# Identity on chip, k and two blocks' normalised rows turned by transfers, some sums as adding transfers: a long-convolution and FFN kernel in one planned order

## The chip, the cores and the metric

The program runs on one core of one Trainium2 chip. The core has five engines that run their own lists of instructions in order: TensorE (PE, matrix products), VectorE (DVE), ScalarE (ACT), GpSimd (POOL) and SyncE (SP, which here only issues transfers). Sixteen DMA engines move data. Time is device time in microseconds (us) of one execution. The kernel before took 301.45 us as the median of three runs (300.62 to 301.98). The profiled execution is one further run of 300.51 us, of which 298.7 us lie between its first and its last instruction (the span).

## The reference

S = 2048 positions, D = 640 channels, F = 1728, bfloat16 inputs.

```python
def _A_ref(q, k, v, shift_k, ssm_k, ssm_D):        # q is layernorm(A_q)
    k_shift = sum of 4 shifted copies of k, each times its tap shift_k[:, t]
    kv = k_shift * v
    y = causal convolution of kv with ssm_k along S (rfft, product, irfft of length 2S)
    return q * (y + kv * ssm_D)

def _B_ref(x, w_gate, w_up, w_down):
    return (silu(x @ w_gate) * (x @ w_up)) @ w_down

h   = A_q + _A_ref(layernorm(A_q), A_k, A_v, A_shift_k, A_ssm_k, A_ssm_D)
out = h + _B_ref(layernorm(h), B_w_gate, B_w_up, B_w_down)
```

## The kernel before

**Tiling.** The 2048 positions are four blocks of 512 (`NB`, `BLK`); a block's rows lie on 128 partitions, four to a partition (`R`). For block j the kernel computes kv_j (`kv_of`): k is turned on PE by products with an identity (L436), copied from PSUM to SBUF (L438), and the four taps are 20 products per row group with diagonal matrices `diag` (L450), multiplied by v on DVE (L455) or after a copy on ACT (L457, L458). The first column of the turned k is the last one of the block before; it is kept in `halo`.

**Convolution.** It is done in blocks with a transform of length 1024, written as products with a fixed basis `WF` of cosines and sines. `transform` makes the spectrum X_j of kv_j and G_j of the filter block (turned by `g_turned`). It forms two sums over even and odd rows on PE (L301), copies them out (L306), and then adds and subtracts them on DVE (L342 "lo", L339 "hi"). With `minus` (a basis with signs changed, `DIRECT`) PE makes both results itself with twice the products (L325) and DVE has no sums to do; G0 is done so. `window` joins G_j and G_{j-1} to H_j; `mac` adds up the complex products X_i H_{j-i} on DVE (L470, L492, L493). `inverse` forms the difference and the sum of the two halves on DVE (L567, L570), goes back with `WI` on PE (L582), multiplies by the normalised row (L592, with the row's sum as a by-product), adds it to x (L595), and makes the second layer norm's statistics: squares on ACT (L503), and the chain of small operations in `norm` (L510 to L532). `turn_h` normalises the rows (L547), turns them on PE with the identity (L609) and copies them to `hT` (L611).

**FFN.** `ffn(j)` runs seven groups of gate and up columns: per group two weight loads on SP (L626), products of 128x512 (L639), silu on ACT (L645), product with up (L654, L656), and then the products with `wd` (L686). For blocks 0 to 2 the block's h is first stored to the output, and the FFN's result is added to it in DRAM by a transfer with accumulation on POOL's queue (L698). The last block adds on DVE (L692) and stores from SP (L696).

**Order.** Nothing is issued when its line is reached. Every line records an operation in a `Plan`, with an engine, an assumed duration, what it reads and writes, and a priority set by `plan.line`. `Plan.schedule` then takes, again and again, the operation that can start first by its own assumed times (ties by priority), gives it a buffer of its tag (`slots`), and so writes the order of each engine's list. Buffers, and so the waits on them, follow from that order. For block j the priority is 10 j, and the FFN of block j-1 has its PE part at 10 j + 15, so it fills PE beside the convolution of block j. The identity is a constant in DRAM that is loaded on ACT's queue behind the taps (L702, L703).

Of the kernel before, what the change touches and what calls it, by code (L numbers as in the profile page):

```python
# [31 lines left out]
FLEX, DIRECT, ACTLN, ACTKV, ENDDVE = 100, ('G0',), 12, 12, True  # L32
SPLIT = ((0,), (1,))

# [34 lines left out]
class Plan:  # L69
    ISSUE = {"sp": 450, "add": 1300}  # L70
    QUEUE = {"add": "pool"}
# [8 lines left out]
    def line(self, at, **own):  # L80

        self.all, self.at = at, own
# [23 lines left out]
    def schedule(self):  # L106
        free = {"sp": 700.0, "aq": 700.0}
        idle = {t: [(0.0, i) for i in range(n)] for t, n in self.slots.items()}
        dma_free = 0.0
        todo = list(self.ops)  # L110
        order = []
        while todo:
            best = None
            for op in todo:
                if any(d.end is None for d in op.deps):
                    continue
# [3 lines left out]
                for b in op.bufs:  # L120
                    if b.tag is not None and b.at is None:
# [7 lines left out]
                        ready = max(ready, sorted(idle[b.tag])[n - 1][0])  # L129
                if not ok:  # L130
                    continue
                for way, late in [((op.eng, op.ns, op.fn), 0.0)] + ([(op.other, 1e3)] if op.other else []):
# [4 lines left out]
                    key = (at, op.prio + late, op.n)  # L137
                    if best is None or key < best[0]:
                        best = (key, op, way)
            if best is None:  # L140
                for op in todo[:60]:
                    print(op.n, op.eng, [(b.tag, b.at) for b in op.bufs], [d.n for d in op.deps if d.end is None])
                print({t: len(idle[t]) for t in idle})
# [6 lines left out]
            for b in op.bufs:  # L150
                if b.tag is not None and b.at is None:
                    idle[b.tag].sort()
                    b.at = idle[b.tag].pop(0)[1]
                    if b.tag in self.turn:
                        self.turn[b.tag].pop(0)
            op.start = start
            if op.eng in self.ISSUE:
                free[self.QUEUE.get(op.eng, op.eng)] = start + self.ISSUE[op.eng]
                dma_free = max(dma_free, start + self.ISSUE[op.eng]) + op.ns
                op.end = dma_free + 1600  # L160
# [8 lines left out]
            order.append(op)  # L169
        order.sort(key=lambda o: (o.start, o.n))  # L170
# [5 lines left out]
def kernel(ctx: ExitStack, tc: tile.TileContext, A_q, A_k, A_v, A_shift_k, A_ssm_k, A_ssm_D, B_x,  # L176
# [7 lines left out]
    slots = {"S": 8, "scr": 3, "x": 2, "ld": 3, "kT": 1, "t4": 2, "hT": 1, "tT": 1, "wgu": 2, "row": 4, "o": 1, "sg": 3,  # L184
             "ps_c": 2, "ps_f": 2, "sm": 4}
    shape = {"S": ([P, 2, 4, D], BF16), "scr": ([P, 4, D], BF16), "x": ([P, R, D], BF16), "ld": ([P, R * D], BF16),
             "kT": ([P, KT, R, P + 2], BF16), "t4": ([P, R, D], BF16), "hT": ([P, KT, BLK], BF16),
# [19 lines left out]
    def conv_ps():  # L207

        turns[0] ^= 1
        return new("ps_f" if plan.all < 2 and turns[0] else "ps_c")  # L210
# [13 lines left out]
    def evict(fn, r, w, ns=700, other=820):  # L224

        return plan.add("act", ns, lambda: fn(nc.scalar.copy), r, w, (),
                        ("dve", other, lambda: fn(nc.vector.tensor_copy)) if plan.all < FLEX else None)
# [4 lines left out]
    def load(nbytes, fn, w, r=()):  # L232
        return plan.add("sp", nbytes / 300.0, fn, r, w)

# [17 lines left out]
    id_h = nc.inline_tensor(np.eye(P, dtype=np.float32).astype(ml_dtypes.bfloat16), name="const_ident")  # L252
# [6 lines left out]
    halo = fixed([P, KT, R, 1], BF16, "halo")  # L259
# [53 lines left out]
    def transform(src, dst, pieces, minus=None):  # L313
# [19 lines left out]
        for ws in () if minus else pieces:  # L333
# [10 lines left out]
            dve(wide(1490, ws), lo, [odd], [(dst, bits((0,), ws=ws))])  # L344
# [42 lines left out]
    def spectrum(src, pieces=((0, 1),), minus=None):  # L387
        b = new("S")
        transform(src, b, pieces, minus)
        return Spec(b)  # L390

    def window(G, prev, to):

        H = Spec(new("S")) if to is None else Spec(to.b, True)
        dve(1490, lambda: nc.vector.tensor_add(H.part(0), G.part(0), prev.part(1)), [G.at(0), prev.at(1)], [H.at(0)])
# [28 lines left out]
    def kv_of(j, k, v):  # L424

        kT = new("kT")
        if j == 0:
            dve(60, lambda: nc.vector.memset(ap(kT)[:, :, :, 0:1], 0.0), [], [(kT, "halo")])
        else:
            dve(100, lambda: nc.vector.tensor_copy(ap(kT)[:, :, :, 0:1], ap(halo)), [halo], [(kT, "halo")])  # L430
        for r in range(R):
            pt = conv_ps()

            def tr(r=r, pt=pt):
                for c in range(KT):
                    nc.tensor.transpose(turned(pt)[:, c * P:(c + 1) * P], rd(k)[:, r, c * P:(c + 1) * P], ap(ident))  # L436
            pe(290, tr, [k, ident], [pt], [kT])
            evict(lambda copy, r=r, pt=pt: copy(  # L438
                ap(kT)[:, :, r, 1:P + 1], turned(pt)[:, 0:D].rearrange("p (c t) -> p c t", c=KT)), [pt], [(kT, r)], other=490)
# [361 lines left out]
```

## Time and profile before

| what | us |
|---|---|
| median of three runs | 301.45 (300.62 to 301.98) |
| the profiled execution | 300.51 |
| its span, first to last instruction | 298.7 |
| PE busy in it | 276.9 (93%) |
| DVE busy | 227.2 (76%) |
| ACT busy | 176.8 (59%) |
| POOL busy | 27.2 (9%) |
| first product on PE starts | 7.79 |
| first FFN product on PE starts | 57.45 |
| FFN of the last block starts on PE | 249.60 |
| last product's result is read by DVE | 295.13 |

Busy time counts stretches in which an engine executes; a group's mean is the length of one instruction, and neighbouring ones overlap on PE, so that 540 products of 379 ns make 122.9 us and not 204.7. The granted TensorE clock was 1.000 throughout. Idle time of an engine matters only where another one, or the end, waits for it.

### The profile page before, as it was taken

The numbers are of one execution on the slowest core, as the hardware profiler recorded it, in microseconds if no ns is written. First come the engines' busy times: TensorE is split into PE (matmuls) and PEld (weight loads), VectorE is DVE, ScalarE is ACT, GpSimd is POOL, SyncE is SP. The second block draws the span as 40 slices with busy tenths as digits, with TensorE's granted clock in tenths as the row PEclk, the third lists the DMA queues.
The fourth block names the chain that finished last, engine by engine and source line by source line (L and its number), as shares of the span: only waits on it lengthen the run. The fifth ranks groups of instructions, "written<-read, shape, count | busy, mean of one in ns | idle before, by whom it ended". The sixth has DMA issues, their size and how long they took to land.

```text
span 298.7 us, 4920 instructions
## 1 busy us (share of the span) xinstructions
PE 276.9 (93%) x1964; PEld 170.0 (57%) x1964; DVE 227.2 (76%) x315; ACT 176.8 (59%) x299; POOL 27.2 (9%) x58
## 2 busy tenths in 40 slices
PE   0899866799999999999999999999999998999995
PEld 0786644665555676665576456654446664444563
DVE  0579998998899989999698999997999871110212
ACT  1848869797775757878768644455453534544300
POOL 0000000362100001126200002110000121000000
PEclk9999999999999999999999999999999999999999
DMA  7999122517536357226242561335555232654011
GB/s 266 373 333 383 49 81 88 178 14 243 170 101 156 102 162 192 34 22 138 81 115 54 150 171 22 37 55 151 150 137 133 25 36 39 170 145 96 2 44 44
DMA packets 52089, 36.91 MB, mean 124 GB/s; under 512 B 12705, under 2 KB 49762, under 8 KB 52066
## 3 DMA queue, kind: packets, MB, share of 16 engines
q1 hardware_dynamic: 49538, 34.59, 39.5%
q0 software_dynamic: 1728, 1.97, 5.7%
q8 instruction: 15, 0.25, 0.4%
q10 hardware_dynamic: 800, 0.04, 0.2%
q14 instruction: 8, 0.07, 0.1%
HBM read 32.00 MB, written 4.59 MB: 122 GB/s over the span
## 4 chain that ended last, share of the span: by engine, by line
PE 85%; DVE 8%; ACT 3%; DMA 2%; issue 1%; ACTq 0%; DVEq 0%
PE ps_f L639 38%; PE ps_f L686 21%; PE ps_c L301 8%; PE ps_c L450 6%; PE ps_c L582 4%; DMA ident<-const_ident 2%; PE ps_f L325 1%; PE ps_c L325 1%; PE ps_f L450 1%; PE ps_c L609 1%; ACT hT L611 1%; DVE row L592 1%; DVE S L470 1%; DVE diag L715 1%; PE ps_c L354 1%; PE ps_c L436 1%
## 5 line engine op out<-in xcount | busy, mean ns | idle before, releaser
L639 PE MATMUL ps_f<-hT,wgu 128*128 128x512 bf16 x540 | 122.9, 379 | 0.7 <-DVE hT L611 0.7
L639 PEld LDWEIGHTS <-wgu 128*128 128x128 bf16 x540 | 52.0, 98 | 57.0 <-issue 0.8
L686 PE MATMUL ps_f<-wd,tT 128*128 128x320 bf16 x448 | 66.3, 300 | 0.2
L686 PEld LDWEIGHTS <-tT 128*128 128x128 bf16 x448 | 41.6, 97 | 22.4 <-issue 7.2
L645 ACT ACTIVATE sg<-ps_f 128x1024 bf16<-128x1024 f32 (+1 forms) x28 | 26.9, 962 | 26.8 <-PE ps_f L639 26.7
L656 DVE TENSOR_TENSOR tT<-sg,sg 128x1024 bf16<-128x1024 bf16 (+1 forms) x27 | 17.5, 649 | 30.7 <-ACT sg L654 30.4
L493 DVE TENSOR_TENSOR S<-S,scr 128x2560 bf16<-128x2560 bf16 x24 | 35.8, 1492 | 0.8
L654 ACT CAST sg<-ps_f 128x1024 bf16<-128x1024 f32 (+1 forms) x27 | 25.5, 946 | 17.5 <-PE ps_f L639 17.4
L301 PE MATMUL ps_c<-t,WF 128*128 128x320 bf16 x208 | 33.9, 299 | 2.0 <-DVE row L592 1.3
L492 DVE TENSOR_TENSOR scr<-S,S 128x2560 bf16<-128x2560 bf16 x24 | 35.6, 1484 | 0.0
L301 PEld LDWEIGHTS <-WF 128*128 128x128 bf16 x224 | 21.5, 98 | 14.1 <-issue 3.7
L503 ACT ACTIVATE row<-x 128x640 bf16<-128x640 bf16 x32 | 23.5, 740 | 8.0 <-DVE x L595 7.4
L698 POOL DMA_DIRECT2D out_dram<-o x12 | 10.6, 883 | 154.5 <-ACT o L694 154.5
L450 PEld LDWEIGHTS <-kT 128*128 128x128 bf16 x320 | 21.4, 107 | 3.1 <-DVE kT L438 1.2
L306 ACT CAST scr<-ps_c 128x640 bf16<-128x640 f32 (+1 forms) x28 | 17.9, 672 | 5.0 <-PE ps_c L301 5.0
L306 ACT CAST S<-ps_c 128x640 bf16<-128x640 f32 (+1 forms) x22 | 13.7, 660 | 10.2 <-PE ps_c L301 10.2
L450 PE MATMUL ps_c<-diag,kT 128*128 128x128 bf16 x280 | 18.3, 226 | 0.2 <-ACT hT L611 0.2
L582 PEld LDWEIGHTS <-WI 128*128 128x128 bf16 x128 | 12.4, 98 | 9.3 <-issue 3.6
L592 DVE SCALAR_TENSOR_TENSOR row<-row,ps_c 128x640 bf16<-128x640 bf16 x14 | 11.5, 819 | 3.2 <-PE ps_c L582 2.6
L611 ACT COPY hT<-ps_c 128x640 bf16<-128x640 bf16 x12 | 8.1, 695 | 9.5 <-PE ps_c L609 9.5
L694 ACT CAST o<-ps_f 128x640 bf16<-128x640 f32 x12 | 8.3, 693 | 8.9 <-PE ps_f L686 7.2
L539 ACT ACTIVATE row<-x 128x640 bf16<-128x640 bf16 x16 | 11.8, 740 | 1.2 <-DMA x<-in_A_q_dram 1.2
(93 smaller groups left out, 293.5 us busy)
## 6 DMA issues: line engine op xcount, KB each, us to landing
wgu<-in_B_w_gate_dram SPq DMA_DIRECT2D x24, 320.0 KB, 3.4
wgu<-in_B_w_up_dram SPq DMA_DIRECT2D x24, 320.0 KB, 3.2
ld<-in_A_k_dram SPq DMA_DIRECT2D x4, 640.0 KB, 4.1
x<-in_A_q_dram SPq DMA_DIRECT2D x4, 640.0 KB, 5.2
ld<-in_A_v_dram SPq DMA_DIRECT2D x4, 640.0 KB, 6.8
ld<-in_A_ssm_k_dram SPq DMA_DIRECT2D x4, 640.0 KB, 6.7
wd<-in_B_w_down_dram SPq DMA_DIRECT2D x1, 2080.0 KB, 11.1
out_dram<-x SPq DMA_DIRECT2D x3, 640.0 KB, 3.8
```

The costliest lines, as they stand in the source:

```text
L301: nc.tensor.matmul(ap(ps)[:, w, 0:NH], ap(WF)[:, r, c, :], ap(src)[:, r, w * NH:(w + 1) * NH], start=(i == 0), stop=(i == 1))
L306: copy(two(cut(to(c)[2](), ws)) if len(ws) == 2 else cut(to(c)[2](), ws), half(ap(ps)) if len(ws) == 2 else ap(ps)[:, ws[0], 0:NH])
L450: nc.tensor.matmul(line(ap(ps))[:, c * P:(c + 1) * P], ap(kT)[:, c, q, off:off + P], ap(diag)[:, 4 * c + t, :], start=(t == 0), stop=(t == 3))
L492: nc.vector.tensor_mul(flat2(b), X.part(xs), H.part(hs))
L493: f(A.part(dst), A.part(dst), flat2(b))
L503: act(930, lambda r=r, junk=junk: nc.scalar.activation(ap(junk), ap(x)[:, r, :], ACT.Square, scale=D ** -0.5, accum_out=sm(s, 1)[:, r:r + ...
L582: nc.tensor.matmul(ap(ps)[:, w, 0:NH], m, src[:, w * NH:(w + 1) * NH], start=(i == 0), stop=(i == len(terms) - 1))
L639: nc.tensor.matmul(ap(ps)[:, i, :], ap(w)[:, k, off:off + P], ap(hT)[:, k, :], start=(k == 0), stop=(k == KT - 1))
L645: act(580 * n + 20 if n == 1 else 1010, lambda: nc.scalar.activation(ap(sg)[:, 0:n, :], ap(gate[0])[:, gate[1]:gate[1] + n, :], ACT.Silu), ...
L654: nc.scalar.copy(ap(co)[:, 0:n, :], ap(up[0])[:, up[1]:up[1] + n, :])
L656: op.rest = dve(420 if n == 1 else 690, lambda: nc.vector.tensor_mul(ap(tT)[:, c:c + n, :], ap(sg)[:, 0:n, :], ap(co)[:, 0:n, :]), [sg, co ...
L686: nc.tensor.matmul(ap(ps)[:, hf, 0:NH], ap(tT)[:n, c, r * P:(r + 1) * P], ap(wd)[:n, c, hf * NH:(hf + 1) * NH], start=(c == 0), stop=(c == ...
```

## The change

It has these parts.

- **Identity.** No longer loaded: DVE sets a tile to one, POOL keeps its diagonal (L806, L807). The taps move to the head of SP's queue (L805), ahead of k.
- **k by transfers.** For blocks 1 to 3, four transfers per block that transpose on the way write k turned into `kT` (L465); block 0 is still turned on PE (L476). `kT` has two buffers; the column from the block before is copied by POOL (L487), and `halo` and its copies on DVE are gone.
- **Rows of blocks 2 and 3 by transfers.** `turn_h` issues a transposing transfer per row (L664) in place of L609 and L611.
- **Sums by adding transfers** on POOL's queue (`add_into`, L260): the "lo" sum for G1, X1, G2 and X2, the sum of the window for H2, and x + row for block 2's four rows.
- **Norms on GpSimd**: the second layer norm of blocks 1 and 2.
- **More by PE alone**: block 0's inverse is in `DIRECT` (64 products in place of 32, no sums on DVE).
- **ACT as first choice** for normalising the rows of block 1 in the convolution, for block 1's copy before the product with v, and for the rows of the second norm of blocks 2 and 3.
- **The last block's last row** of the output is finished in two halves of 320 columns.
- **Order.** Each stage of each block gets its own offset to its priority (`PLACE`); the planner's assumed times for transfers change, a buffer that was taken counts from when it came free, and, of several operations that could start first on an engine, one with a priority lower by 5 or more is taken. `SLOTS`: x from 2 to 1, ld 3 to 2, kT 1 to 2, row 4 to 5, o 1 to 3, sm 4 to 6. `ROWS` are worked off as 1, 3, 0, 2.
- `LEAD`, `ADDMAC` and `WAIT` are empty or zero, so the paths they switch on are not taken.

```diff
-FLEX, DIRECT, ACTLN, ACTKV, ENDDVE = 100, ('G0',), 12, 12, True
+ADDLO, ADDMAC, ADDWIN, ADDH, LEAD = ('G1', 'X1', 'G2', 'X2'), (), (1,), (2,), {}
+PAD = 16
+DIRECT, ACTLN, ACTKV, ACTLN2 = ('G0', 'inv0'), 1, 1, (2, 3)
+LN1DVE, LN2POOL, HTURN = (0,), (2, 1), (2, 3)
+WAIT = {'dve': 0, 'act': 0, 'pe': 0}
+PLACE = {"G0": 14.5, "G1": 2.5, "G2": -71.0, "G3": -15.5, "X0": -14.5, "X1": -10.5, "X2": -13.5, "X3": 15.0,
...
+SLOTS = {"S": 8, "scr": 3, "x": 1, "ld": 2, "kT": 2, "t4": 2, "hT": 1, "tT": 1, "wgu": 2, "row": 5, "o": 3,
+         "sg": 3, "ps_c": 2, "ps_f": 2, "sm": 6}
+ROWS = (1, 3, 0, 2)
...
-    ISSUE = {"sp": 450, "add": 1300}
-    QUEUE = {"add": "pool"}
+    ISSUE = {"sp": 450, "turn": 1260, "add": 870}
+    QUEUE = {"turn": "sp", "add": "pool"}
...
+            best = min(found, key=lambda f: f[0]) if found else None
+            if best:
+                until = best[0][0] + WAIT.get(best[2][0], 0)
+                best = min((f for f in found if f[2][0] == best[2][0] and f[0][0] <= until and (f[0][1] <= best[0][1] - 5 or f is best)),
+                           key=lambda f: (f[0][1] // 5, f[0][0], f[0]))
...
+    def add_into(to, what, r, w, n=R * D):
+
+        plan.add("add", 2 * P * n * 2 / 375.0, lambda: nc.gpsimd.dma_start(
+            out=to(), in_=what(), accum_op=ALU.add, max_dma_last_dim=2 * D * 2), r, w)
...
             dve(wide(1490, ws), hi, [odd, (dst, bits((0,), ws=ws))], [(dst, bits((1,), ws=ws))])
-            dve(wide(1490, ws), lo, [odd], [(dst, bits((0,), ws=ws))])
+            if name in ADDLO:
+                add_into(lambda: ap(dst)[:, 0], lambda odd=odd: ap(odd), [odd], [(dst, bits((0,)))])
+            else:
+                dve(wide(1490, ws), lo, [odd], [(dst, bits((0,), ws=ws))])
...
+        if to and ADDWIN:
+            add_into(lambda: prev.part(1), lambda: G.part(0), [G.at(0), prev.at(1)], [H.at(0)])
+        else:
+            dve(1490, lambda: nc.vector.tensor_add(H.part(0), G.part(0), prev.part(1)), [G.at(0), prev.at(1)], [H.at(0)])
...
+    def load_k(j):
+
+        kT = new("kT")
+        if j == 0:
+            load(MB, lambda: nc.sync.dma_start(out=plain(kT), in_=block(kk, j)), [kT])
+        for r in range(R) if j else ():
+            plan.add("turn", MB / 4 / 300.0, lambda r=r: nc.sync.dma_start(
+                out=ap(kT)[:, :, r, PAD:], in_=block(kk, j)[:, r, :], transpose=True), [], [(kT, r)])
+        return kT
...
-            dve(100, lambda: nc.vector.tensor_copy(ap(kT)[:, :, :, 0:1], ap(halo)), [halo], [(kT, "halo")])
+            plan.add("pool", 900, lambda: nc.gpsimd.tensor_copy(ap(kT)[:, :, :, PAD - 1:PAD], ap(before)[:, :, :, PAD + P - 1:]),
+                     [(before, r) for r in range(R)], [(kT, "halo")])
...
+                if plan.block in ADDH:
+                    add_into(lambda r=r: ap(x)[:, r, :], lambda t=t: ap(t), [t], [(x, r)], D)
+                else:
+                    dve(490, lambda r=r, t=t: nc.vector.tensor_add(ap(x)[:, r, :], ap(x)[:, r, :], ap(t)), [t], [(x, r)])
...
-        norm(s, nc.vector, n1)
+            norm(s, nc.gpsimd if plan.block in LN2POOL else nc.vector, n1, bias=True, rs=sorted(rs))
...
+            if plan.block in HTURN:
+                plan.add("turn", MB / 4 / 300.0, lambda hn=hn, at=at: nc.sync.dma_start(
+                    out=ap(hT)[:, :, at * P:(at + 1) * P], in_=ap(hn), transpose=True), [hn], [(hT, r)])
+                continue
...
+            last = end and r == ROWS[-1]
+            for lo, hi in zip(cuts, cuts[1:]):
+                for hs in ((0,), (1,)) if last else ((0, 1),):
...
-    plan.add("aq", 1900, lambda: nc.scalar.dma_start(out=ap(tapw), in_=A_shift_k.rearrange("(c p) t -> p c t", p=P)), [], [tapw])
-    plan.add("aq", 1900, lambda: nc.scalar.dma_start(out=ap(ident), in_=id_h.ap()), [], [ident])
-    k = load_t(kk, 0)
+    load(1e3, lambda: nc.sync.dma_start(out=ap(tapw), in_=A_shift_k.rearrange("(c p) t -> p c t", p=P)), [tapw])
+    dve(100, lambda: nc.vector.memset(ap(ident), 1.0), [], [ident])
+    plan.add("pool", 1500, lambda: nc.gpsimd.affine_select(ap(ident), ap(ident), [[-1, P]], ALU.is_equal, 0.0, base=0, channel_multiplier=1), [], [ident])
+    k = load_k(0)
```

## The prediction

> **What bounds the kernel now.** I read the page's busy times and slices first, then the busy time of four stretches, the start's timeline, the end of block 0's convolution, and the groups that the change touches.
>
> ```profile
> PE 276.9 (93%) x1964; PEld 170.0 (57%) x1964; DVE 227.2 (76%) x315; ACT 176.8 (59%) x299; POOL 27.2 (9%) x58
> ...
> PE   0899866799999999999999999999999998999995
> ```
>
> ```profile
> core 0: us, PE busy (x) PEld busy (x) DVE busy (x) ACT busy (x) POOL busy (x), PEclk, DMA share, GB/s
> ...
> 7.80:57.40 49.60, 40.64 (x365) 31.10 (x365) 43.01 (x83) 39.06 (x89) 0.49 (x2) 1.00 0.63 215
> 57.40:226.00 168.60, 168.52 (x1191) 100.70 (x1189) 157.58 (x183) 111.51 (x176) 23.07 (x49) 1.00 0.46 113
> 226.00:295.20 69.20, 67.75 (x414) 38.12 (x412) 25.79 (x50) 24.96 (x36) 3.48 (x4) 1.00 0.32 72
> ```
>
> There are two regimes. To 57.4 us the kernel waits for loads and then walks block 0's chain through DVE, ACT and PE. From there PE is the bound: 0.08 us idle in the third stretch, 1.4 us up to its last product. DVE is nearly full beside it to 226 us (93%) and almost free after.
>
> ```profile
> 4.50 0.10 PEld L436 LDWEIGHTS <-ld 128*128 128x128 bf16 x1 [4.50 <-DMA ld<-in_A_k_dram]
> 7.79 0.69 PE L436 MATMUL ps_f<-ident,ld 128*128 128x128 bf16 x5 [7.79 <-DMA ident<-const_ident]
> 7.84 2.82 DVE L715 TENSOR_TENSOR diag<-ident,tapw 128x2560 bf16<-128x2560 bf16 x1 [6.90 <-DMA ident<-const_ident]
> ...
> 38.55 0.81 DVE L567 TENSOR_TENSOR scr<-S 128x1280 bf16<-128x1280 bf16 x1
> ...
> 47.81 0.49 DVE L595 TENSOR_TENSOR x<-x,row 128x640 bf16<-128x640 bf16 x1
> ...
> 52.07 1.51 DVE L547 TENSOR_SCALAR row<-x,sm 128x640 bf16<-128x640 bf16 x4
> ...
> 57.45 0.81 PE L639 MATMUL ps_f<-hT,wgu 128*128 128x512 bf16 x3
> ```
>
> k is there at 4.50 but the identity only at 7.79; the inverse's sums start on DVE at 38.55, its last row is done at 48.30, the norm at 52.03, the first FFN product starts at 57.45.
>
> ```profile
> L436 PE MATMUL ps_c<-ident,ld 128*128 128x128 bf16 x70 | 6.3, 232 | 0.5 <-ACT scr L306 0.3 <-ACT kT L438 0.2
> L609 PE MATMUL ps_c<-ident,row 128*128 128x128 bf16 x70 | 5.6, 220 | 1.6 <-ACT hT L611 1.6
> L342 DVE TENSOR_TENSOR S<-S,scr 128x2560 bf16<-128x2560 bf16 x5 | 7.5, 1491 | 0.1
> L698 POOL DMA_DIRECT2D out_dram<-o x12 | 10.6, 883 | 154.5 <-ACT o L694 154.5
> q0 software_dynamic: 1728, 1.97, 5.7%
> ```
>
> PE's turning costs 0.08 to 0.09 us a product, a "lo" sum 1.49 us of DVE, an adding transfer 0.88 us of POOL.
>
> **The change, part by part**, against the profiled span of 298.7 us.
>
> *Start.* k is turned when both k and the identity are there. Both are uncertain. k is now queued behind the taps: the identity, 32 KB, queued behind the same taps, landed 6.5 us after its issue, k, 640 KB at the head, 3.8 us after its own; so k lands between 5.0 (0.45 us for one issue more) and about 8.5. The identity needs a memset and one POOL operation. POOL's rows of 128x4 run from 0.19 to 1.5 us, POOL is idle from 0.43 us, and nothing in the trace bounds a first operation there from above, so I put it between 1.5 and 8.5. Turning starts between 5.0 and 8.5 in place of 7.79: a gain of 2.8 to a loss of 0.7. I take 6.8, the middle: **-1.0**. `diag` (2.82 us) goes along, since it too waits for taps and identity.
>
> [...]
>
> *Block 0's inverse on PE alone.* DVE's four sums go (38.55 to 41.82). After the last product sum in `mac`, PE does the second half's first row (8 products of 0.136, 1.1 us), then DVE takes four rows at 1.27 us (43.86, 45.13 in the old spacing): 6.8 us from the end of `mac` to the last row, against 48.30 - 38.55 = 9.75. **-2.9**. The 32 extra products (4.3 us) run while DVE makes the second half's products, where PE idles now (5.54 of 8.0 us busy from 35 to 43); without that cover they would cost up to 2.2 us for one half.
>
> *From the last row to the first FFN product.* The norm began 1.74 us after the last row, behind two copies of 0.82; in the new order two copies of 0.49 stand there: -0.3 after one more small operation of 0.17. From the norm's end to the first product it took 5.4 us, with k's four turnings, their copies and one tap group (1.28) in the way. In the new order four normalisings (1.5), three row copies on ACT (0.70 each) and two basis sums (0.55 each) end last: 4.5. **-1.2** in all. So the first FFN product moves from 57.45 to 52.4.
>
> *PE's work after it.* 1599 products before, 1544 after: 80 turnings less (40 for k, 40 for rows), 25 more that used to lie ahead (20 of the taps, 1.12 us, and 5 turnings of a filter). In full flow a pair of groups of 10 takes 0.73 us, so a turning is worth about 0.056 to 0.09: 80 of them 4.5 to 7.2, less 1.4. I take the low price, since they were interleaved: **-3.2** (to -5.8). All FFN and inverse products are the same ones.
>
> *The end.* The last row's final addition covers 320 columns in place of 640, 0.47 in place of 0.82 (L306's copy of 320 against L692): **-0.35**.
>
> *What waits instead.* PE had 1.4 us idle after the first FFN product. From DVE 14.6 us go there (four "lo" sums and a window sum of 1.49, four additions of 0.49, two norms of 2.0, the halo copies), from PE 3.2, so DVE's work has more room. But five sums of 640 KB are now transfers, and DVE waits for their end. An adding transfer of 160 KB landed 3.4 us after its issue; the queue's share (5.7% of 16 engines over the span, 272 engine-us for 1.97 MB) makes 1.4 us of data for 160 KB and 5.6 for 640, so 7.6 us; the lower end is the plain 640 KB store, 3.8 us. In the new order the places are: G1's sum has some 7 us (four products with v, paced by PE) before DVE needs it; X1's has 6.1 (0.69, two of 1.49, five of 0.49), and POOL does block 1's first norm ahead of it (3.5 and 7.8 us in the two runs before); H2's sum is issued only when G2's has landed, and DVE has 3.7 us of other work (two of 1.49, one of 0.69) before it needs H2. So 0 to 1.5 us of waiting at X1 and 0 to 4 at H2, and 0 to 3 more from POOL's order. Part is absorbed in DVE's room. I put PE's idle time at 3.2, between 0.3 and 9: **+1.8**.
>
> *Covered at nothing.* Block 2's rows: the chain is four adding transfers, squares, a POOL norm (up to 8 us), four ACT rows of 0.92, four turning transfers; PE has about 30 us of FFN work of block 1 left when the inverse ends, and the chain adds to 22 or so. The new order's POOL queue has no DRAM additions between these. Block 3's rows are the tight place: after the inverse PE has three groups of 1.08 and 112 products of 0.144 (16.12 us), some 17.2 us from the last inverse product. The chain: row and addition 1.4, square 0.93, two more small FFN products on ACT and DVE (about 2), norm 2.2, row 0.44, four transfers issued one after another, the landing. Up to the first issue that is 7.0. A turning transfer is not in the trace. Nearest below is a plain load of 160 KB, 0.37 us to issue and 3.6 to land; above, the filter load in 640 pieces, 6.7 us to land. At 1 us apiece and 4 to land it is 15.0, so 2.2 us are left. Block 1's k has over 30 us.
>
> [...]
>
> **Sum:** -1.0 - 2.9 - 1.2 - 3.2 - 0.35 + 1.8 = -6.85, span 291.9, the profiled execution 293.7. The median of the runs shown is 0.94 above the profiled one; I take half of that: 294.1.
>
> **Rivals.** *A: DVE waits for its sums.* If adding transfers take 7.6 us and more beside the weight loads, DVE falls behind by some 2 to 4 us at each of X1, G2 and H2, and PE waits for block 1's and block 2's inverse; idle 7 to 10 in place of 3.2: 298 to 301. For it: DVE at 93% before. Against: 14.6 us less to do.
>
> *B: everything is covered and the start is early.* Turning starts at 5.0 (-1.8 more) and PE idles 0.5 (-2.7 more): 289.6. For it: 0.08 us idle over 168.6 us in the old plan with a fuller DVE.
>
> *C: slower, by turning transfers.* In block 3's hand-over each microsecond per row beyond 1 costs four; 2.2 us are free and 6.85 gained, so from about 3.3 us a row the gain is gone. At the filter load's 6.7 us one after another, the four take 26.8, the FFN of block 3 starts 20.6 us late, and the kernel takes 314 or more. For it: no such row in the trace. Against: a plain load of this size lands in 3.6 with several in flight.
>
> *D: the identity is not earlier* (POOL late, or k behind the taps): the start gives nothing or loses 0.7, 295.1 to 295.8.
>
> **How the numbers follow.** Forecast with D 0.60 (about 292 to 297), B 0.14 (289 to 292), A 0.18 (297 to 301), C 0.08 (from 301). The range 289.2 to 299.6 leaves out about half of A's upper part, C, and a bit of B. Under 0.5% is about what a measurement can't tell from no change (299.9 to 303.0 is "same"): faster 0.87, same 0.05, slower 0.08.
>
> **What would show it.** Start: first product on PE near 6.8, and what it waits for. Inverse: L631 with `minus`, first FFN product near 52.4. PE: 1896 products, busy near 273. Sums: waits of DVE for a transfer into S, and PE idle between 57 and 200. Hand-over: PE waiting for hT from L664 before block 3's first FFN product would be C. The prediction is wrong if transfers into hT or S appear on the chain of work that ended last with more than 5 us.

## The result and the profile after

The changed kernel takes 303.35 us (median of eight, 302.71 to 304.97); the kernel before took 301.65 beside it (300.58 to 302.50). The ratio is 1.0073, with a 95% interval of 1.0044 to 1.0101. It is slower by 0.7%, a little more than the half per cent that the prediction called hardly measurable. 294.1 was forecast, and the measurement lies outside the range.

The profiled execution took 303.14 us, its span is 301.1. From the page of the changed kernel, the busy line, then slices:

```profile
PE 276.1 (92%) x1896; PEld 166.5 (55%) x1896; DVE 206.7 (69%) x269; ACT 174.2 (58%) x291; POOL 98.0 (33%) x103
...
PE   2999989999994999989899996699999999999995
...
POOL 0000101297001499115993798220891022000000
PEclk9999999999998999999999999599999999999999
```

PE has 68 products less, DVE 20 us less to do, and POOL 98.0 us in place of 27.2. PE now has two holes, in slice 13 (about 90 to 98 us) and around slices 25 and 26 (180 to 196), and in both the granted clock drops. POOL is full for some stretch ahead of each. Busy time by stretch of the changed kernel, from the first FFN product on:

```profile
core 0: us, PE busy (x) PEld busy (x) DVE busy (x) ACT busy (x) POOL busy (x), PEclk, DMA share, GB/s
48.30:85.00 36.70, 36.70 (x330) 24.51 (x328) 26.99 (x27) 29.43 (x49) 15.59 (x17) 1.00 0.78 171
85.00:100.00 15.00, 11.15 (x57) 6.06 (x56) 14.06 (x15) 9.20 (x14) 1.20 (x1) 0.89 0.54 108
100.00:180.00 80.00, 77.37 (x535) 46.52 (x533) 72.24 (x79) 52.06 (x87) 50.86 (x51) 1.00 0.59 130
180.00:215.00 35.00, 29.11 (x163) 15.70 (x162) 25.46 (x19) 19.87 (x34) 13.67 (x14) 0.90 0.49 96
215.00:297.58 82.58, 82.50 (x469) 44.32 (x466) 30.54 (x52) 33.58 (x44) 15.06 (x15) 1.00 0.45 97
```

Set against the prediction's terms, by the two profiled executions:

| stretch | before | after | change | forecast |
|---|---|---|---|---|
| to the end of block 0's products on DVE | 38.55 | 34.12 | -4.4 | -1.0 |
| from there to block 0's last row | 9.75 | 6.22 | -3.5 | -2.9 |
| from there to the first FFN product | 9.15 | 7.96 | -1.2 | -1.2 |
| PE busy from the first FFN product to the last product | 236.2 | 236.8 | +0.6 | -3.2 |
| PE idle in that stretch | 1.5 | 12.45 | +11.0 | +1.8 |
| from the last product to the end of the span | 3.57 | 3.52 | -0.05 | -0.35 |

The first FFN product starts at 48.30 where 52.4 was forecast, so the first half went better than foretold. All of it and more went after that. The waits of the changed kernel say at what:

```profile
ACT row L600 <- POOL sm L560: 11.3, 2, 9.4
DVE scr L539 <- DMA S<-scr: 10.5, 2, 5.3
...
PE ps_f L781 <- ACT o L786: 5.9, 1, 5.9
...
PE ps_c L631 <- DVE scr L616: 3.9, 1, 3.9
```

and POOL has come onto the chain that ended last, where it had no share before (first line before, second line changed):

```profile
PE 85%; DVE 8%; ACT 3%; DMA 2%; issue 1%; ACTq 0%; DVEq 0%
PE 52%; DVE 20%; POOL 14%; DMA 6%; ACT 3%; issue 3%; DVEq 0%; SPq 0%; ACTq 0%; POOLq 0%
```

There are two causes of waiting. ACT stands 9.4 us before block 2's rows (L600) because POOL's norm isn't done; the copy of an output of block 1's FFN (L786) is queued behind it on ACT, and PE waits 5.9 us for that copy's PSUM buffer. And DVE stands twice, for 5.3 and 5.2 us, before L539 because X1's and X2's sums, adding transfers, land late; behind the first of these PE waits 3.9 us for block 1's inverse, and the second delays block 2's inverse and so the norm that ACT waits for. Those sums were ready early. X1's was ready to be issued at 68.1 us (the end of L365) but stood on POOL's queue behind a norm until 72.31; X2's, ready at 112.9, stood until 118.86. POOL's timeline of the changed kernel there (start, length):

```profile
59.15 1.41 POOL L560 TENSOR_TENSOR sm<-sm 128x4 f32<-128x4 f32 x1
60.64 1.31 POOL L571 TENSOR_SCALAR sm<-sm 128x4 int32<-128x4 int32 x1
62.04 0.52 POOL L573 TENSOR_TENSOR sm<-sm 128x4 f32<-128x4 f32 x1
62.63 1.32 POOL L578 TENSOR_TENSOR sm<-sm 128x4 f32<-128x4 f32 x1
64.05 1.31 POOL L579 TENSOR_SCALAR sm<-sm 128x4 f32<-128x4 f32 x1
...
72.31 1.24 POOL L260 DMA_DIRECT2D S<-scr  x1
```

and DVE's in the same microseconds:

```profile
59.00 1.49 DVE L517 TENSOR_TENSOR S<-S,S 128x2560 bf16<-128x2560 bf16 x1
60.41 1.49 DVE L428 TENSOR_TENSOR S<-S,S 128x2560 bf16<-128x2560 bf16 x1
61.82 0.68 DVE L739 TENSOR_TENSOR tT<-sg,sg 128x1024 bf16<-128x1024 bf16 x1
62.42 2.88 DVE L517 TENSOR_TENSOR scr<-S,S 128x2560 bf16<-128x2560 bf16 x2
```

An operation on 512 numbers takes POOL 1.3 us there: it ends 0.13 to 0.15 us after DVE starts its next instruction (60.56 after 60.41, 61.95 after 61.82). In these rows POOL gets through one operation for each large instruction of DVE. DVE itself isn't slowed: L539 takes 1484 ns in the mean, the same 1484 as its counterpart L492 before. This norm took 13.6 us, the second norm of block 1 15.6 (103.31 to 118.91) and that of block 2 20.0 (167.06 to 187.03). The prediction had 3.5 to 8.

### The profile page after: what moved, and what is told of

Read it like the earlier page. It is cut to its first block, busy times and chain, and to the rows that moved or that the text cites. A ratio compares the mean times of both kernels' runs of the same rounds, so it can differ in the third digit from the quotient of the medians.

```text
span 301.1 us, 4828 instructions
## 1 busy us (share of the span) xinstructions
PE 276.1 (92%) x1896; PEld 166.5 (55%) x1896; DVE 206.7 (69%) x269; ACT 174.2 (58%) x291; POOL 98.0 (33%) x103
## 4 chain that ended last, share of the span: by engine, by line
PE 52%; DVE 20%; POOL 14%; DMA 6%; ACT 3%; issue 3%; DVEq 0%; SPq 0%; ACTq 0%; POOLq 0%
PE ps_f L713 20%; PE ps_f L781 14%; DVE scr L539 6%; DVE S L540 5%; PE ps_c L631 5%; DMA S<-scr 5%; POOL sm L578 3%; PE ps_c L327 3%; POOL sm L580 2%; PE ps_c L497 2%; POOL sm L573 2%; POOL sm L579 2%; PE ps_f L748 2%; DMA kT<-in_A_k_dram 2%; PE ps_f L351 1%
## 5 line engine op out<-in xcount | busy, mean ns | idle before, releaser
L713 PE MATMUL ps_f<-hT,wgu 128*128 128x512 bf16 x480 | 108.4, 379 | 1.5 <-ACT sg L737 1.5
L713 PEld LDWEIGHTS <-wgu 128*128 128x128 bf16 x480 | 46.7, 98 | 54.0 <-issue 2.3
L539 DVE TENSOR_TENSOR scr<-S,S 128x2560 bf16<-128x2560 bf16 x24 | 35.6, 1484 | 10.6 <-DMA S<-scr 10.5
L550 ACT ACTIVATE row<-x 128x640 bf16<-128x640 bf16 x32 | 23.4, 733 | 15.8 <-DVE x L651 13.6
L787 POOL DMA_DIRECT2D out_dram<-o x12 | 10.5, 898 | 52.2 <-ACT o L786 52.2
L631 PEld LDWEIGHTS <-WI 128*128 128x128 bf16 x144 | 14.5, 102 | 12.3 <-DVE scr L616 4.3
L600 ACT ACTIVATE row<-x,sm 128x640 bf16<-128x640 bf16 x17 | 14.7, 914 | 11.3 <-POOL sm L560 11.3
L332 ACT CAST scr<-ps_c 128x640 bf16<-128x640 f32 (+1 forms) x30 | 19.5, 674 | 2.4 <-PE ps_c L327 2.3
L497 PEld LDWEIGHTS <-kT 128*128 128x128 bf16 x320 | 18.8, 100 | 1.5 <-DVE kT L478 0.7
L260 POOL DMA_DIRECT2D S<-scr x4 | 5.1, 1269 | 39.8 <-DVE S L365 39.8
L786 ACT CAST o<-ps_f 128x640 bf16<-128x640 f32 x12 | 8.2, 692 | 16.6 <-PE ps_f L781 15.8
L497 PE MATMUL ps_c<-diag,kT 128*128 128x128 bf16 x280 | 16.6, 219 | 0.0
L559 POOL TENSOR_SCALAR sm<-sm 128x4 f32<-128x4 f32 x12 | 9.5, 790 | 15.1 <-ACT row L550 13.8
```

The source lines that it names most:

```text
L332: copy(two(cut(to(c)[2](), ws)) if len(ws) == 2 else cut(to(c)[2](), ws), half(ap(ps)) if len(ws) == 2 else ap(ps)[:, ws[0], 0:NH])
L497: nc.tensor.matmul(line(ap(ps))[:, c * P:(c + 1) * P], ap(kT)[:, c, q, off:off + P], ap(diag)[:, 4 * c + t, :], start=(t == 0), stop=(t == 3))
L539: nc.vector.tensor_mul(flat2(b), X.part(xs), H.part(hs))
L550: act(930, lambda r=r, junk=junk: nc.scalar.activation(ap(junk), ap(x)[:, r, :], ACT.Square, scale=D ** -0.5, accum_out=sm(s, 1)[:, r:r + ...
L631: nc.tensor.matmul(ap(ps)[:, w, 0:NH], m, src[:, w * NH:(w + 1) * NH], start=(i == 0), stop=(i == len(terms) - 1))
L713: nc.tensor.matmul(of(ps, i), ap(w)[:, k, off:off + P], ap(hT)[:, k, lo:lo + n], start=(k == 0), stop=(k == KT - 1))
```

## The experiments

Theory T1: the five norms on POOL are slow beside DVE's large instructions, and what stands behind them (sums on POOL's own queue, rows on ACT) makes PE wait. Rivals: T2, the adding transfers themselves make DVE late; T3, the new order or the smaller buffers lose the time. Ratios are against runs of the kernel before on the same chip; a difference of two ratios is put into microseconds with 301.

### The norms, the sums, and the plan

The plan is a list written ahead of time, so an operation can be given to another engine while its place stays the same. For the norms:

```diff
     def norm(s, v, mean=None, bias=False, rs=range(R)):
+        planned, v = v, nc.vector
...
-        plan.add("dve" if v is nc.vector else "pool", 2400 if v is nc.vector else 7500, go, ...
+        plan.add("dve" if planned is nc.vector else "pool", 2400 if planned is nc.vector else 7500, go, ...
```

> The plan stays as it is, with the same order and the same buffers; only the five norms that stood on POOL (the first norms of blocks 1 to 3, the second ones of blocks 1 and 2) are made by DVE at the places the plan gave them. Theory T1 (slow POOL norms, 13 to 19 us each beside DVE's sums, hold up the sums queued behind them and ACT's rows): the waits of DVE for X1's and X2's sum shrink to under 2 us each, ACT's 9.4 us wait at L600 goes, PE's idle time from the first FFN product to the last product falls from 12.6 to about 3 and the clock loss of some 3.7 us with it: 291 to 295 us. Rival T2 (the adding transfers themselves, about 7 us from issue to landing, make DVE late): DVE still waits about 5 us at X1 and X2, only ACT's wait goes: 296 to 299. Rival T3 (the new order or the single slot of x loses the time): 301 to 304.

Measured: **292.01 us**, ratio 0.9710 (0.9686 to 0.9734). By stretch, up to and from the first FFN product:

```profile
0.00:48.55 48.55, 40.02 (x352) 30.12 (x353) 36.58 (x79) 30.04 (x66) 1.57 (x7) 1.00 0.91 252
48.55:286.69 238.14, 233.69 (x1546) 135.66 (x1543) 176.18 (x240) 144.01 (x226) 20.23 (x22) 1.00 0.57 125
```

PE's idle time falls from 12.45 to 4.45 us, and the same products take 233.7 instead of 236.8 us with no drop of the clock. ACT's wait at L600 is gone, DVE's at L539 for the transfers is 2.5 us in place of 10.5 (1.3 more at the window's sum). So T1, and not T3: order and buffers are those of the changed kernel. The five norms on POOL cost 10.9 us, and without them the change is worth 2.9%.

The sums, the same way:

```diff
+        def transfer():
+            if n == D:
+                nc.gpsimd.dma_start(out=to(), in_=what(), accum_op=ALU.add, ...)
+            else:
+                nc.vector.tensor_add(to(), to(), what())
-        plan.add("add", ..., lambda: nc.gpsimd.dma_start(...), r, w)
+        plan.add("add", ..., transfer, r, w)
```

> The plan stays as it is; the five sums of 640 KB (G1, X1, G2, X2 and the window's) are made by DVE at their places instead of by adding transfers, the norms stay on POOL. T1: DVE no longer waits for transfers, but has 7.5 us more to do (five of 1.49), ACT still waits about 9 us for the second norm of block 2 and PE about 6 us behind it: 298 to 302. T2: the loss is gone: 293 to 297. T3: 301 to 304.

Measured: 296.63, ratio 0.9860 (0.9837 to 0.9884), 1.4 us below T1's range and inside T2's. ACT still waits 9.4 us and PE 5.9 behind it, as T1 had it; what T1 had too small was the price of the late sums.

> Both edits together: no norm on POOL and no sum of 640 KB by transfer, same order. DVE has about 18 us more than the changed kernel and is about as full as before the change. T1 and T2 both: 291 to 296, with PE idle under 5 us after the first FFN product. T3: 300 or more.

Measured: 293.42, ratio 0.9753 (0.9734 to 0.9771). Together the four ratios are:

| | sums by transfer | sums by DVE |
|---|---|---|
| norms on POOL | 1.0073 | 0.9860 |
| norms on DVE | 0.9710 | 0.9753 |

Adding transfers are worth 1.3 us where no norm stands ahead of them on POOL's queue (the two intervals just touch), and cost 6.4 us where the norms do. That settles T2: a transfer's landing of some 7 us (with the norms on DVE 6.5 in the median of the four "lo" sums, 8.4 for the window's) is covered but for the 2.5 and 1.3 us above, if it is issued at once. With the sums on DVE, the norms on POOL still cost 3.2 us, by ACT's rows.

> The norms stay on POOL, the sums stay transfers; only the planner's assumed price of a POOL norm goes from 7.5 to 14 us, so that it may lay other work around it. T1, if the wrong price is the fault and the work can be laid around it: 295 to 300, with ACT's wait at L600 under 4 us. T1, if a POOL norm of 13 to 19 us can't be covered by any order: 301 to 305. T2: 301 to 305, since X1's and X2's transfers still land about 7 us after their issue.

```diff
-        ... 2400 if v is nc.vector else 7500, go, ...
+        ... 2400 if v is nc.vector else 14000, go, ...
```

Measured: 311.22, ratio 1.0348 (1.0329 to 1.0366), worse than any expectation. The second norm of block 2 takes 21.8 us in the new order (174.14 to 195.95), and PE stands 17.8 us for the transfers of block 2's rows. Telling the planner a time nearer to the truth did not help here.

### What slows a POOL operation, and which norms count

```diff
+    def in_halves(f, *t):
+        for i in range(2):
+            f(*(a[:, i] for a in t))
...
-                nc.vector.tensor_mul(flat2(b), X.part(xs), H.part(hs))
-                f(A.part(dst), A.part(dst), flat2(b))
+                in_halves(nc.vector.tensor_mul, flat2(b), X.part(xs), H.part(hs))
+                in_halves(f, A.part(dst), A.part(dst), flat2(b))
```

(and the same for the six instructions of a first product)

> The changed kernel with every norm where it was, on POOL. Only DVE's instructions of 128x2560 in the complex products (L517, L539, L540) are issued as two of 128x1280, 66 more of them; a half takes 0.82 us where a whole one takes 1.49, so DVE has about 6 us more to do. Theory P (a POOL operation beside a large DVE instruction ends only when that instruction ends): a POOL operation of 128x4 beside the halves takes 0.65 to 0.85 us instead of 1.3 to 1.45, the norms of 13 to 19 us take 8 to 11, and the kernel gets faster although DVE does more: 296 to 301 us. Rival M (POOL is slowed by DVE's traffic as such, however it is cut): norms of 13 to 19 us as before, and the 6 us more of DVE show: 304 to 308.

Measured: 312.58, ratio 1.0386 (1.0353 to 1.0419). The total speaks for neither, the rows for P, and for something worse. POOL's timeline with halved products:

```profile
64.21 0.66 POOL L584 TENSOR_TENSOR sm<-sm 128x4 f32<-128x4 f32 x1
64.94 0.66 POOL L577 TENSOR_TENSOR sm<-sm 128x4 f32<-128x4 f32 x1
65.68 0.66 POOL L582 TENSOR_TENSOR sm<-sm 128x4 f32<-128x4 f32 x1
...
174.67 0.80 POOL L563 TENSOR_SCALAR sm<-sm 128x4 f32<-128x4 f32 x1
175.55 19.33 POOL L564 TENSOR_TENSOR sm<-sm 128x4 f32<-128x4 f32 x1
```

DVE's rows beside them, and the first and last beside the long operation:

```profile
63.26 3.02 DVE L512 TENSOR_TENSOR scr<-S,S 128x1280 bf16<-128x1280 bf16 x4
...
175.63 1.54 DVE L512 TENSOR_TENSOR scr<-S,S 128x1280 bf16<-128x1280 bf16 x2
...
193.27 1.54 DVE L512 TENSOR_TENSOR S<-S,scr 128x1280 bf16<-128x1280 bf16 x2
```

Beside halves of 0.82 us an operation takes 0.66 where it took 1.31, so it is the length of DVE's instruction that counts and not its traffic. But the last operation of block 2's second norm took 19.33 us: from 175.63 to 194.81 DVE ran 26 halves without a gap, and the operation ended at 194.88, when DVE had run out of work. It missed every boundary on the way; why it did, when others of its kind got through, is open. ACT then stood 21.3 us and PE 17.7. The block's norm took 32.4 us. The changed kernel has a smaller case: one operation of 4.46 us across three large instructions (113.36 to 117.82).

The operations of 1.31 and 0.66 us ended just after the start of DVE's next instruction; what ties the two together was not shown.

The two kinds of norm apart (in the first edit, only norms with `mean`, then only those without):

> Same plan and order; only the second norms of blocks 1 and 2 are made by DVE, the first norms of blocks 1 to 3 stay on POOL. If the two second norms carry the loss (ACT's wait of 9.4 us at L600 and PE's 5.9 behind it, X2's late sum): 293 to 296. If the first norm of block 1 ahead of X1's sum carries half of it (DVE waits 5.3 us, PE 3.9): 296 to 299.

> Same plan and order; only the first norms of blocks 1 to 3 are made by DVE, the second norms of blocks 1 and 2 stay on POOL. X1's sum is issued some 13 us earlier; X2's stays behind the second norm of block 1, and ACT waits for the second norm of block 2. If the second norms carry the loss: 299 to 302. If the first ones carry half: 296 to 299.

Measured: 293.82, ratio 0.9771 (0.9736 to 0.9805), with only the second norms on DVE; 300.95, ratio 0.9987 (0.9966 to 1.0008), with only the first ones. So the second norms of blocks 1 and 2, which the change moved, carry 9.1 us, and the first ones, which were on POOL before, 2.6. The two add up to 11.7, near the 10.9 measured together.

### The parts that went well

```diff
-    load(1e3, lambda: nc.sync.dma_start(out=ap(tapw), ...), [tapw])
-    dve(100, lambda: nc.vector.memset(ap(ident), 1.0), [], [ident])
-    plan.add("pool", 1500, lambda: nc.gpsimd.affine_select(...), [], [ident])
+    load(1e3, lambda: nc.scalar.dma_start(out=ap(tapw), ...), [tapw])
+    load(1e3, lambda: nc.scalar.dma_start(out=ap(ident), in_=id_h.ap()), [ident])
```

(with all norms on DVE)

> All norms on DVE as in the first run of this study (292.0 us), and the start as it was before the change: taps and identity loaded on ACT's queue, k at the head of SP's. If the start passes through to the end: first product on PE at 7.8 instead of 5.5, first FFN product 2 to 4 us later (the higher value if the slow first tap products of the kernel before, 2.62, 2.34 and 2.07 us for 20, come back as well), 294 to 296. If the start is hidden by what follows: 291.5 to 292.5.

Measured: 297.36, ratio 0.9876 (0.9855 to 0.9898), above the 294 to 296 expected: the new start is worth 5.0 us, and -1.0 was forecast. The first product starts at 7.87 instead of 5.45, the first FFN product at 51.86 instead of 48.55. 1.6 us more lie in PE's products after that, with a granted clock of 0.94 between 100 and 130 us, where PE is idle for 1.8 us (1.6 in the same stretch with the new start, at 1.00); why is open.

With all norms on DVE and `DIRECT` without `'inv0'`:

> All norms on DVE as in the first run of this study (292.0 us), and block 0's inverse no longer by PE alone: 32 products less there, DVE makes the sums and differences of the halves again. The plan is made anew, so the total may also move by order; what is read here is local. If the prediction's price of 2.9 us for this part is right: the first FFN product starts 2 to 4 us later than 48.6, at 50.6 to 52.6. If the sums are hidden on DVE: 48.6 to 49.6. Total: 294 to 302, by how well the new order falls.

Measured: 299.45, ratio 0.9931 (0.9907 to 0.9956). The first FFN product starts at 51.31 in its one profiled execution, 2.8 us later than with `'inv0'` (48.55). The prediction asked 2.9 for this part. But this execution took 302.4 us, 3 us above the median, and its granted clock up to 51.31 was 0.97 where it was 1.00 with `'inv0'`, so it can't confirm the price. The plan was made anew, and the total loss of 6.7 us can't be put down to this part.

With all norms on DVE and `HTURN = ()`:

> All norms on DVE as in the first run of this study, and the rows of blocks 2 and 3 turned by PE and copied from PSUM again, with no transposing transfers for them; the plan is made anew. If PE's time for a turning (0.056 to 0.09 us for each of 40) is what the transfers are worth: PE's busy time rises by 2.2 to 3.6 us and the kernel takes 294 to 297. If the transposing transfers' own landing (3.7 us, four issues of 1.3 us) costs as much at block 3's hand-over: 291 to 293.

Measured: 295.88, ratio 0.9847 (0.9809 to 0.9885). PE is busy 1.4 us longer after the first FFN product (2.2 to 3.6 expected) and idle 1.3 us longer, and that product comes 1.2 us later. Turning block 2's and 3's rows by transfers is worth some 4 us, of which part may be order. The transfers land in 3.7 us (median, 2.6 to 6.8) and are issued 1.25 us apart in the changed kernel, and PE never waits for them there.

### Parts done alone on the kernel before

The same two lines in the kernel before, for its first norms (POOL to DVE) and for the second norms of blocks 1 and 2 (DVE to POOL):

```diff
+        planned, v = v, nc.vector
...
+        planned, v = v, nc.gpsimd if mean and 10 <= plan.all < 30 else v
```

> The kernel before, same plan and order, only the first norms of blocks 1 to 3 made by DVE instead of POOL. If a POOL norm costs only where something is queued behind it: no change, 300.5 to 302.5 (three norms of about 2.4 us more on a DVE that is 93% full may cost up to 2). If POOL's norms slowed the kernel before as well: 296 to 299.

> The kernel before, same plan and order, only the second norms of blocks 1 and 2 made by POOL instead of DVE: this part of the change done alone. Beside DVE's large instructions a POOL norm takes 10 to 19 us, but where DVE itself stands and waits for it, its operations take 0.2 us and the norm about 4. If DVE's row normalisings are queued soon behind: two waits of 4 to 6 us in place of two norms of 2, 303 to 309. If DVE has much other work ahead of them, up to 15 us each: 310 to 325. If this part costs nothing without the new order: 300.5 to 302.

Measured: 304.11, ratio 1.0108 (1.0090 to 1.0126), and 301.22, ratio 1.0008 (0.9989 to 1.0027). The first misses both of its ranges. The second falls in the range for a part that costs nothing, but its norms are shorter than the 10 to 19 us expected beside DVE's work. POOL was the right place for the first norms in the kernel before: DVE is so full there (93% from 57.4 to 226 us) that some 2 us more for each of them leaves PE 5.1 us idle after the first FFN product in place of 1.5; two new waits of 1.3 us for DVE (63 and 79 us) stand out. And the second norms alone on POOL cost nothing. In that order they take 8.2 and 6.6 us (103.20 to 111.43, 167.78 to 174.37). POOL's rows in the second case:

```profile
105.17 0.52 POOL L519 TENSOR_TENSOR sm<-sm 128x4 f32<-128x4 f32 x1
105.78 0.23 POOL L513 TENSOR_SCALAR sm<-sm 128x4 f32<-128x4 f32 x1
106.09 0.20 POOL L514 TENSOR_TENSOR sm<-sm 128x4 f32<-128x4 f32 x1
106.38 0.19 POOL L522 TENSOR_SCALAR sm<-sm 128x4 int32<-128x4 int32 x1
```

From 105.64 to 107.75 DVE waits for ACT, and POOL runs at 0.2 us an operation. What a POOL norm costs is thus set by what DVE has been given to do beside it. That leaves the question whether the planner, by laying work there, makes the norm slow.

The kernel before again, now with a plan that knows of the two norms and lays 10 us of work beside each:

```diff
-        norm(s, nc.vector, n1)
+        norm(s, nc.gpsimd if 10 <= plan.all < 30 else nc.vector, n1)
```

> The kernel before with the second norms of blocks 1 and 2 on POOL, as in the run before it (301.2 us), but the plan knows it and lays 10 us of other work beside each in place of 2. If the work laid beside a POOL norm is what slows it: norms of 10 to 18 us instead of 8.2 and 6.6, and 303 to 310 us. If planning for it helps: 298 to 301, with norms of 6 to 9.

Measured: 302.16, ratio 1.0036 (1.0016 to 1.0056). The norms take 13.5 us (102.31 to 115.83) and 12.8 (167.17 to 179.92): work laid beside a norm lengthens it, as expected. The price in time is only 0.8 us against the run before, not clear of noise (the two intervals overlap), and the 303 to 310 were too high. No sums stand behind the norms on this kernel's POOL queue; whether that is the whole reason was not tried apart.

The changed kernel with its norms planned at 3 us:

> The changed kernel with its five norms on POOL, planned at 3 us instead of 7.5 (303.35 us), so that what needs them is queued soon behind them. If the work laid beside a POOL norm slows it, whoever needs it now stands and waits sooner where that is DVE, and the norm gets shorter: second norms of 5 to 10 us instead of 15.6 and 20.0, and 294 to 300 us. Where ACT needs it (block 2's rows) DVE goes on, and that norm stays at 12 us and more: then 299 to 304. If the planned time doesn't matter: 302 to 305.

Measured: 302.16, ratio 1.0038 (1.0023 to 1.0053). The second norm of block 1 keeps its place and its 15.6 us, and DVE its 10.5 us of waiting for sums. That of block 2 takes 14.0 instead of 20.0, and ACT waits 5.1 instead of 9.4. That is the case in which ACT needs the norm and DVE goes on. No price told to the planner (3, 7.5 or 14) brought the kernel with its norms on POOL below 302.

The first norms of blocks 2 and 3 back on POOL, the other three norms on DVE:

```diff
+        planned, v = v, nc.vector if mean or plan.block < 2 else v
```

> The changed kernel's plan and order; both norms of block 1 and the second norm of block 2 on DVE, the first norms of blocks 2 and 3 left on POOL. Beside the run with all five on DVE (292.0): DVE has about 5 us less to do. If nothing waits for these two: 290 to 292. If DVE's rows or sums wait for one of them: 292 to 295.

Measured: **291.60**, ratio 0.9711 (0.9675 to 0.9748), the same as with all five on DVE. These two take 13 us and more, and no wait of another engine for a POOL norm is left. Both versions beat both kernels by about 3% or more.

This also shows which first norm costs: with all three on POOL the kernel takes 293.82 (the run with the second norms on DVE), with block 1's on DVE as well 291.60 (ratios 0.9771 and 0.9711, whose intervals just overlap). Block 1's is the one that stands ahead of X1's sum.

## Why the prediction was wrong, point by point

**The step that failed is "What waits instead", put at +1.8 (PE idle 3.2 us, "between 0.3 and 9"); measured are 12.45 us of idle time and 3.1 us more for the same products at a lower clock.** Within it, the number that failed is the time of a POOL norm, "3.5 and 7.8 us in the two runs before", and "up to 8 us" in the chain of block 2's rows. Those were whole norms (there are three; the third, from 136.99, took 7.3), taken in places where DVE happened to stand idle for part of the time. The price was in the trace before, one level lower. POOL's rows of the kernel before:

```profile
139.32 1.32 POOL L523 TENSOR_TENSOR sm<-sm 128x4 f32<-128x4 f32 x1
140.72 1.45 POOL L528 TENSOR_TENSOR sm<-sm 128x4 f32<-128x4 f32 x1
142.26 0.19 POOL L529 TENSOR_SCALAR sm<-sm 128x4 f32<-128x4 f32 x1
142.53 0.20 POOL L530 TENSOR_TENSOR sm<-sm 128x4 f32<-128x4 f32 x1
```

and DVE's beside them:

```profile
139.10 1.48 DVE L492 TENSOR_TENSOR scr<-S,S 128x2560 bf16<-128x2560 bf16 x1
140.62 1.49 DVE L493 TENSOR_TENSOR S<-S,scr 128x2560 bf16<-128x2560 bf16 x1
144.64 0.69 DVE L656 TENSOR_TENSOR tT<-sg,sg 128x1024 bf16<-128x1024 bf16 x1 [2.52 <-ACT sg L654]
```

1.32 and 1.45 us while DVE is at work, 0.19 and 0.20 in DVE's gap from 142.11 to 144.64. The prediction quoted this spread ("from 0.19 to 1.5 us") for the identity and did not ask what makes it. A norm of 14 to 16 operations at 1.4 us from start to start is 20 to 22 us, the upper price that was missing (the 4.46 us of one operation show that even this is no firm bound). It would have put the chain of block 2's rows at 22 - 8 + 20, some 34 us, against "about 30 us" of cover, and X1's and X2's sums 6 to 12 us later. The path was wrong too. PE never waited for block 2's rows: it stopped within the cover, because the copies of block 1's FFN outputs stand behind those rows on ACT. The prediction also named that "POOL does block 1's first norm ahead of" X1's sum, but gave it 0 to 1.5 us of waiting at X1 and 0 to 3 more for POOL's order; DVE waited 5.3 us at X1 and 5.2 at X2. The start, better by 3.4 us than foretold, hid part of this.

**DVE "has more room" was true and did not help.** It is POOL's norms that need the gaps. DVE's busy time after the first FFN product fell from 183 to 169 us, but the large instructions around the norms stand back to back.

**Block 0's inverse, -2.9:** measured -3.5, right. **Last row to first FFN product, -1.2:** measured -1.2, right.

**Start, -1.0:** measured -4.4 to the end of block 0's products. The first product came 1.9 us earlier (5.93, waiting for k). The tap products no longer wait 0.64 us for `diag` (0.48 for `kT` now), and they run at full speed (1.28 us for 20) sooner, which the trace before could not tell; part of that differs from run to run, see the last section. The identity's operation on POOL took 0.29 us at 1.14 us, so the identity was there at 1.43, ahead of k; no run shows the 8.5 that the prediction took as its upper end.

**PE's work, -3.2:** with the norms out of the way -2.5 (236.2 to 233.7); right in kind, a little large. **The end, -0.35:** -0.05.

**Block 3's hand-over, covered with 2.2 us to spare:** right. PE does not wait for its rows.

**Rivals.** A (298 to 301, DVE waits for its sums) has the right symptom and the wrong cause: the same transfers, landing in 6.7 us in the median, cost 2.5 us of waiting at L539 when no norm stands ahead of them. The prediction's sign of being wrong, transfers into S with over 5 us of the last chain, did show (7.14 and 6.61 us, 5% of the span); but they have 5% as well in the run with the norms on DVE, which takes 292.01, so the sign does not tell the cause. B and D fell: the start was early, but not everything was covered. C fell: turning transfers land in 3.7 us. The forecast was off the measurement by 9.3 us, and the norms on POOL cost 10.9; the other terms came within 1 us (PE's work counted with the norms on DVE), but for the start.

## What to carry to other kernels

Before work is moved to GpSimd, take the length of one of its operations beside the DVE instructions that will run there, not the mean of a group nor a whole routine from another place; here it was 0.2 us in DVE's gaps, 1.3 beside a 1.49 us sum, and 19.33 at worst. Then look at what is queued behind it, on GpSimd's own queue (transfers count: X1's sum stood there from 68.1 to 72.31 us) and on the engine that waits for it. Cover did not help such operations where it was DVE's work (on the kernel before, two norms of 8.2 and 6.6 us took 13.5 and 12.8 with more of it beside them); giving five such routines to DVE in the same places cost DVE some 2 us each (block 1's first ran from 60.66 to 62.66) and won 10.9.

## What the runs showed of the hardware

**The price of a wait of PE can be more than the wait.** The first row after PE's wait of 3.85 us, and the one after its wait of 5.89 us, in the changed kernel's timeline of PE, with rows of as many products of the same lines that no wait precedes:

```profile
94.81 3.99 PE L631 MATMUL ps_c<-scr,WI 128*128 128x320 bf16 x16 [3.85 <-DVE scr L616]
...
162.22 2.33 PE L631 MATMUL ps_c<-S,WI 128*128 128x320 bf16 x16
...
176.03 8.08 PE L781 MATMUL ps_f<-wd,tT 128*128 128x320 bf16 x56
...
191.19 9.60 PE L781 MATMUL ps_f<-wd,tT 128*128 128x320 bf16 x56 [5.89 <-ACT o L786]
```

16 products take 3.99 us in place of 2.33, and 56 take 9.60 in place of 8.08. The granted clock is 0.57 during the one row and 0.84 during the other. In three runs in which the first row waited only 1.60 to 2.09 us (norms on DVE, first norms on DVE, late first norms on POOL), it took 2.35, and in the first and the last of them the clock is 1.00 from the first FFN product to the last product. So there the short waits cost no more than themselves, and the one of 3.85 us did; at what length the loss begins was not shown. Nor is such a wait all that lowers the clock: with the identity loaded it was 0.94 between 100 and 130 us, where PE was idle for 1.8 us in all.

**At the start PE is slow for a time that differs.** Kernel before, tap products in groups of 20:

```profile
10.72 2.62 PE L450 MATMUL ps_f<-diag,kT 128*128 128x128 bf16 x20 [0.64 <-DVE diag L715]
13.13 2.34 PE L450 MATMUL ps_c<-diag,kT 128*128 128x128 bf16 x20
15.27 2.07 PE L450 MATMUL ps_f<-diag,kT 128*128 128x128 bf16 x20
17.18 1.28 PE L450 MATMUL ps_c<-diag,kT 128*128 128x128 bf16 x20
```

and the changed kernel:

```profile
8.83 1.77 PE L497 MATMUL ps_f<-diag,kT 128*128 128x128 bf16 x19 [0.48 <-DVE kT L478]
10.44 1.28 PE L497 MATMUL ps_c<-diag,kT 128*128 128x128 bf16 x20
```

Full speed, 1.28 us for 20, comes 9.4 us after the first product (7.79) in the one and 4.5 (5.93) in the other, with a granted clock shown as 1.00 in both. These two executions lie near the ends of a spread. In the four profiled runs with the old kernel's start it comes after 7.1 to 9.4 us, in the twelve with the new start after 4.2 to 6.8, and eight of these, which share one plan, span that whole range; with the identity loaded in the changed kernel it is 7.3. The first product with `WF`, behind the taps, starts at 13.79 in the changed kernel's execution and at 14.28 in the mean of those eight; before, at 18.29, and at 17.9 in the mean of the four. So some 0.9 us of the -4.4 is the draw of two executions. What makes the difference was not tried and stays open.
